# Turning the first MLP block's rows by crossbar DMA transposes instead of TensorE products and ScalarE copies

## The chip, the cores and the metric

The kernel runs on one core of a Trainium2 chip. The metric is the device time of one execution in microseconds (us). Engines are named as the profile names them: PE (TensorE products), PEld (its weight loads), DVE (VectorE), ACT (ScalarE), POOL (GpSimd) and SP (SyncE, which in this kernel only issues DMAs).

## The reference

Four residual layers run over 2048 tokens of width 576: attention, MLP, attention, MLP, with the same weights for both attention layers and for both MLP layers.

```python
def _A_ref(x, wqkv, wo):              # linear attention, 32 heads of 18
    q, k, v = split(x @ wqkv)
    phi = lambda t: jnp.where(t > 0, t + 1, jnp.exp(t)) + 1e-6
    kv = einsum("bhsd,bhse->bhde", phi(k), v);  z = phi(k).sum over s
    o = einsum(phi(q), kv) / (einsum(phi(q), z) + 1e-6)
    return o @ wo
def _B_ref(x, w1, b1, w2, b2):        # MLP, hidden width 4608
    y = _layernorm(x)
    return gelu(y @ w1 + b1) @ w2 + b2

x = A_x
x = x + _A_ref(_layernorm(x), A_wqkv, A_wo)
x = x + _B_ref(_layernorm(x), B_w1, B_b1, B_w2, B_b2)
x = x + _A_ref(_layernorm(x), A_wqkv, A_wo)
x = x + _B_ref(_layernorm(x), B_w1, B_b1, B_w2, B_b2)
```

Inputs, weights and output are bfloat16.

## The kernel before

**Layout.** Tokens lie in 16 row tiles of 128 (`t`), four of them make a block of 512 tokens (`c`). The layers are numbered from 1 here; the code's `li` counts from 0, so that layers 2 and 4 (the MLPs) are `li` 1 and 3, and the attention layers that feed them `li` 0 and 2. The products of each layer need the normalized rows with the width on the partitions: that is `yT`, five chunks of 128 by 2048 tokens. The fifth chunk has only 64 real values; for an MLP they are there twice, which is why GpSimd copies the last 64 columns of a normalized row once more behind them (L476).

**Row pipe.** `LNPipe` takes a residual row tile through stages, one stage a tick: statistics (stage 0, on DVE, or on ACT in two steps, L379 and L388), the reciprocal root (L433), a scale and shift (L436), the normalization into one of three row buffers `y_ring` (L466 where GpSimd does it), and then the turning of the row (stage 4). A tile can be made to `hold` for a number of ticks. There are two ways of turning. With `evac="act"` five TensorE transposes (L500) go to a PSUM bank `tp` and one ScalarE copy (L505) takes them to `yT`. With `evac="dma"` the rows are turned in 32x32 squares by VectorE into `turned`, stored to DRAM (L310), and fetched into place, a block of four tiles at a time.

**The handover from attention to MLP.** In the last stage of an attention layer `wo_stage(t)` makes the output product of row tile t in a pair of PSUM banks, `accA` for even t and `accB` for odd (L933), `residual` adds the old residual row `xo` on VectorE (L605), and the new row is stored to DRAM (L612). The old rows are loaded ahead by `prefetch_xo`, in layer 1 as pairs from the input (L575), in layer 3 one by one (L581), each into one of nine row buffers. Row tiles 0 to 3 go straight into the row pipe with `evac="act"`, normalized by GpSimd; their transposes come at an output row that is written out by hand (`tp_at`). One or two ticks follow each output row.

**The MLP.** For each block of 512 tokens, `m1_group` makes four hidden chunks at a time (L1045): two go to banks `h_ps` first, then two to a pair `hp_ps`, for which the banks `accA` and `accB` take turns, `accA` first. Each product takes all four row tiles of the block as its moving operand. Then the second product runs over all 36 hidden chunks for each row tile (L1104). Rows of blocks 1 to 3 are loaded again (L372) while the block before is computed, and are turned with `evac="dma"`.

**Order.** TensorE's order in the last attention stage and in the MLP is the program's, held by a chain of dependencies. On the other engines and on SP the tile framework's planner orders instructions by their dependencies and its own costs, within some orders set by hand. SP issues in that order and waits at each DMA for what it needs, so that a DMA that is not ready keeps those behind it back.

Of the kernel before, what the change touches and what calls it, by code (L numbers as in the profile page):

```python
# [15 lines left out]
P = 128  # L16
# [19 lines left out]
def build(tc, A_x, A_wqkv, A_wo, B_w1, B_b1, B_w2, B_b2, out, dbg=None, n_layers=4):  # L36
    nc = tc.nc
    dbg = dbg or {}
    with ExitStack() as ctx:
# [307 lines left out]
        class LNPipe:  # L347
# [11 lines left out]
            def tick(self, transposes=1):  # L359
                land()  # L360
                for it in list(self.items):
                    st = it["stage"]
                    if st == 4 and it["evac"] != "dma":
                        if transposes == 0 or state["wo"] < it["tp_at"]:
                            continue
                        transposes -= 1
# [57 lines left out]
                    elif st == 1:  # L424
                        rstd = work.tile([P, 1], F32, name="ln_rstd", bufs=6)
                        it["rstd"] = rstd
                        if "u" not in it:
                            named(f"ln{it['t']}", nc.scalar.activation(out=rstd[:], in_=it["mv"][:, 1:2], func=ACT.Ln,
                                                                       bias=eps_col[:, 0:1]))
                            named(f"re{it['t']}", nc.scalar.activation(out=rstd[:], in_=rstd[:], func=ACT.Exp, scale=-0.5))  # L430
                            it["stage"] = 2
                            continue
                        nc.gpsimd.tensor_tensor(out=rstd[:], in0=it["u"][:], in1=neg_half[:], op=ALU.pow)  # L433
                    elif st == 2 and it["norm"] != "dve":
                        nmr = work.tile([P, 1], F32, name="ln_nmr", bufs=4)
                        nc.gpsimd.tensor_scalar(out=nmr[:], in0=it["mv"][:, 0:1], scalar1=1.0 if it["stats"] == "act" else -1.0,  # L436
                                                scalar2=it["rstd"][:, 0:1], op0=ALU.mult, op1=ALU.mult)
                        it["nmr"] = nmr
                    elif st in (2, 3) and it["kind"] == "A" and it["evac"] == "act":
                        xt, t = it["xt"], it["t"]  # L440
                        tail = first_tail(t)[:, 0:64]
                        if it["norm"] == "pool":
                            for out, cols in ((xt[:, 0:4 * P], slice(0, 4 * P)), (tail, slice(4 * P, D))):
                                norm = nc.gpsimd.tensor_scalar(out=out, in0=xt[:, cols], scalar1=it["rstd"][:, 0:1],
                                                               scalar2=it["nmr"][:, 0:1], op0=ALU.mult, op1=ALU.add)
                            pool_last["norm"] = norm.ins.name
                        else:
                            for name, out, cols in ((f"n{t}", xt[:, 0:4 * P], slice(0, 4 * P)), (f"nt{t}", tail, slice(4 * P, D))):
                                norm = named(name, nc.vector.tensor_scalar(
                                    out=out, in0=xt[:, cols], scalar1=it["mv"][:, 0:1], scalar2=it["rstd"][:, 0:1],  # L450
                                    op0=ALU.subtract, op1=ALU.mult))
                            dve_last["norm"] = norm.ins.name
                        row_of[t] = xt
                        it["stage"] = 4
                        continue
                    elif st in (2, 3):
                        if sum(other["stage"] == 4 for other in self.items) == NY:
                            continue
                        y = y_ring[state["ycnt"] % NY]
                        state["ycnt"] += 1  # L460
                        xt = it["xt"]
                        if it["norm"] == "act":
                            nc.scalar.activation(out=y[:, 0:D], in_=xt[:, 0:D], func=ACT.Identity,
                                                 scale=it["rstd"][:, 0:1], bias=it["nmr"][:, 0:1])
                        elif it["norm"] == "pool":
                            norm = nc.gpsimd.tensor_scalar(out=y[:, 0:D], in0=xt[:, 0:D], scalar1=it["rstd"][:, 0:1],  # L466
                                                           scalar2=it["nmr"][:, 0:1], op0=ALU.mult, op1=ALU.add)
                            pool_last["norm"] = norm.ins.name
                        else:
                            norm = nc.vector.tensor_scalar(out=y[:, 0:D], in0=xt[:, 0:D], scalar1=it["mv"][:, 0:1],  # L470
                                                           scalar2=it["rstd"][:, 0:1], op0=ALU.subtract, op1=ALU.mult)
                            if it["after"] == "phi":
                                tc.add_manual_dep(norm.ins, dve_last["phi"], NOSYNC, reason="keys go on first")
                            dve_last["norm"] = norm.ins.name
                        if it["kind"] == "B" and it["evac"] != "dma":
                            nc.gpsimd.tensor_copy(out=y[:, D:DPAD], in_=y[:, 4 * P:D])  # L476
                        if it["kind"] == "A" and it["evac"] == "dma":
                            c, j = divmod(it["t"], TPC)
                            nc.sync.dma_start(out=yrow_d[c, :, j], in_=y[:, 0:D])
                        it["y"] = y  # L480
                        it["stage"] = 4
                        continue
                    elif st == 4:
                        t = it["t"]
                        first_layer = it["kind"] == "A" and it["evac"] == "act"
                        y = it["xt"] if first_layer else it["y"]
                        if it["evac"] == "dma":
                            turn_rows(y, t, it["kind"])
                            self.items.remove(it)
                            continue  # L490
                        tp = ps_h.tile([P, 512], F32, name="tp", tag="h")
                        tp = tp[:, 0:DPAD // 2].bitcast(BF16).rearrange("p (k n) -> p k n", k=KD)
                        first = first_layer and t < 2
                        tp2 = tp
                        if first:
                            tp2 = ps_h.tile([P, 512], F32, name="tp2", tag="h")
                            tp2 = tp2[:, 0:DPAD // 2].bitcast(BF16).rearrange("p (k n) -> p k n", k=KD)
                        for k in range(KD):
                            block = first_tail(t, P) if first_layer and k == 4 else y[:, k * P:(k + 1) * P]
                            pe(nc.tensor.transpose(out=(tp if k < 3 else tp2)[:, k, :], in_=block, identity=ident[:]))  # L500
                        if first:
                            named(f"ca{t}", nc.scalar.copy(out=yT[:, 0:3, t * P:(t + 1) * P], in_=tp[:, 0:3, :]))  # L502
                            named(f"cd{t}", nc.vector.tensor_copy(out=yT[:, 3:KD, t * P:(t + 1) * P], in_=tp2[:, 3:KD, :]))
                        elif it["evac"] == "act":
                            turned_tile = nc.scalar.copy(out=yT[:, :, t * P:(t + 1) * P], in_=tp)  # L505
                            act_last["turned"] = turned_tile.ins.name
                            if first_layer and t < 5:
                                named(f"ca{t}", turned_tile)
                            elif act_last["exp"] is not None:
                                tc.add_manual_dep(turned_tile.ins, act_last["exp"], NOSYNC, reason="keys go on first")  # L510
                        else:
                            nc.vector.tensor_copy(out=yT[:, :, t * P:(t + 1) * P], in_=tp)
                        self.items.remove(it)
                        continue
# [6 lines left out]
        lnp = LNPipe()  # L521
# [93 lines left out]
        def layer_A(li, next_kind, pre_a1=None):  # L615
# [321 lines left out]
            def wo_stage(t):  # L937
# [1 line left out]
                wp = wo_open[t][1]  # L939
                xn = residual(li, t, wp[:, :, 0:HALF])  # L940
                if xn is not None and next_kind == "B" and t < TPC:
                    lnp.feed(xn, t, "B", "pool", "act", hold=(2, 5, 6, 8)[t] if li > 0 else (2, 8, 8, 10)[t], tp_at=6 + 2 * t if li > 0 else (6, 10, 11, 14)[t],
                             **(dict(after="sum") if t in (0, 3 if li > 0 else 2) else dict(stats="act", after="rden")))

            for t in range(AHEAD if li == 0 else AHEAD + 2):
# [267 lines left out]
```

## Time and profile before

| | |
|---|---|
| device time, median of 3 runs | 760.16 us (760.14 to 760.37) |
| span of the profiled execution | 758.4 us |
| busy: PE, PEld | 753.2 us, 487.4 us |
| busy: ACT, DVE, POOL | 328.7 us, 272.0 us, 116.6 us |
| transposes of layer 2's and 4's first block (L500) | 40, median 218 ns |
| all copies from `tp` to `yT` by ACT (L505) | 22, median 687 ns (8 of them for these rows) |
| DMA | 73.90 MB, mean 97 GB/s |

The profile is of one execution, with times in us from the start of its span; the page gives no other time of its own for it, and the span is 1.8 us under the median. Busy times of engines overlap. A PE instruction's duration contains its way through the array, so the room that one takes in a row of products is the distance of two starts. In a timeline a row gives the start, the length, the engine, the line, the operation with its output and inputs, the count of merged instructions, and in brackets the idle time before it and what ended it.

### The profile page before, as it was taken

Reading aid. Unit: us, or ns where it says so; the run is one execution under the profiler, and the core shown is the slowest. Engines: PE = TensorE matmul, PEld = TensorE weight load, DVE = VectorE, ACT = ScalarE, POOL = GpSimd, SP = SyncE. Lnnn points to the kernel's source line nnn. Section 1 sums busy time; section 2 is a strip of 40 time slices with the busy share of each in tenths; the row PEclk is TensorE's granted clock in tenths of the full one; section 3 lists DMA queues with packets and bytes.
Section 4 is the critical chain, followed back from the end, with each engine's and each line's share of the span. In section 5 each row is a group of like instructions: output and inputs, shape, how many; then the busy total and the mean of one; then the engine's idle time right before and its main releaser. Section 6 shows DMA issues by size and latency. Waiting matters only on the chain.

```text
span 758.4 us, 15817 instructions
## 1 busy us (share of the span) xinstructions
PE 753.2 (99%) x6595; PEld 487.4 (64%) x6595; DVE 272.0 (36%) x685; ACT 328.7 (43%) x733; POOL 116.6 (15%) x196
## 2 busy tenths in 40 slices
PE   9999999999999999999999999999999999999998
PEld 5776754774477457646777777457646754774476
DVE  8876862136033503401367577600230131000000
ACT  6887656205600650263057666660174036205600
POOL 4840231002000301200100005300020020001000
PEclk9999999999999999999999999999999999999999
DMA  8994573026312711320404047530240033011000
GB/s 236 267 313 74 178 262 82 17 64 189 83 39 83 181 51 48 109 69 17 131 24 116 24 136 255 185 82 16 88 115 7 16 127 82 9 33 55 1 9 24
DMA packets 80977, 73.90 MB, mean 97 GB/s; under 512 B 36874, under 2 KB 65546, under 8 KB 80906
## 3 DMA queue, kind: packets, MB, share of 16 engines
q1 hardware_dynamic: 80906, 72.90, 33.0%
q8 instruction: 51, 0.84, 0.5%
q14 instruction: 20, 0.16, 0.1%
HBM read 48.10 MB, written 24.77 MB: 96 GB/s over the span
## 4 chain that ended last, share of the span: by engine, by line
PE 97%; DVE 1%; ACT 0%; issue 0%; DVEq 0%
PE m_ps L1104 36%; PE h_ps L1045 21%; PE hp_ps L1045 16%; PE q_ps L621 6%; PE k_ps L653 5%; PE wo_ps L933 5%; PE k_ps L678 4%; PE m_half L1104 1%; PE tp L500 1%; PE warm_ps L217 1%; PE k_tail L678 1%; PE kv_ps L719 0%; PE den_ps L769 0%; PE rden_ps L810 0%; PE kvwo_half L737 0%
## 5 line engine op out<-in xcount | busy, mean ns | idle before, releaser
L1104 PE MATMUL m_ps<-w_sb,hT 128*128 128x288 bf16 x2232 | 274.8, 286 | 0.0
L1104 PEld LDWEIGHTS <-hT 128*128 128x128 bf16 x2304 | 224.3, 98 | 60.4 <-issue 3.4
L1045 PEld LDWEIGHTS <-w_sb 64*128 64x128 bf16 x2304 | 124.5, 94 | 136.4 <-issue 1.9
L1045 PE MATMUL hp_ps<-yT,w_sb 64*128 64x512 bf16 x1152 | 178.0, 376 | 0.0
L1045 PE MATMUL h_ps<-yT,w_sb 64*128 64x512 bf16 x1152 | 148.0, 376 | 0.0
L1050 ACT COPY relay_sb<-relay_sb 128x1 f32<-128x1 f32 x144 | 28.5, 198 | 260.4 <-PE h_ps L1045 217.6
L1041 ACT ACTIVATE hT<-h_ps,b1T 128x512 bf16<-128x512 f32 x144 | 91.0, 683 | 44.1 <-PE h_ps L1045 44.1
L433 POOL TENSOR_TENSOR ln_rstd<-ln_u,neg_half 128x1 f32<-128x1 f32 x61 | 35.2, 577 | 439.9 <-DVE ln_u L415 218.0
L1041 ACT ACTIVATE hT<-hp_ps,b1T 128x512 bf16<-128x512 f32 x144 | 91.1, 692 | 0.0
L605 DVE TENSOR_TENSOR xbf<-m_ps,xo 128x576 bf16<-128x576 f32 x15 | 11.4, 757 | 213.5 <-PE m_ps L1104 213.5
L605 DVE TENSOR_TENSOR xo<-m_ps,xo 128x576 f32<-128x576 f32 x16 | 12.1, 757 | 172.6 <-PE m_ps L1104 172.6
L588 POOL TENSOR_TENSOR xo<-xo,b_bc 128x576 f32<-128x576 f32 x32 | 40.9, 1283 | 97.3 <-DMA xo<-x_d 58.4
L1045 PE MATMUL h_ps<-yT,w_tail 64*128 64x512 bf16 x144 | 54.1, 376 | 0.0
L1045 PE MATMUL hp_ps<-yT,w_tail 64*128 64x512 bf16 x144 | 54.1, 376 | 0.0
L621 PE MATMUL q_ps<-yT,wqkv_sb 128*126 128x512 bf16 (+1 forms) x200 | 49.3, 379 | 0.1
L653 PE MATMUL k_ps<-wqkv_sb,yT 128*128 128x288 bf16 x320 | 44.6, 286 | 0.2
L933 PE MATMUL wo_ps<-kvwo,pq 126*128 126x288 bf16 (+1 forms) x320 | 43.4, 286 | 0.3
L1045 PEld LDWEIGHTS <-w_tail 64*128 64x128 bf16 x288 | 27.1, 94 | 17.1
L653 PEld LDWEIGHTS <-yT 128*128 128x128 bf16 x320 | 31.0, 98 | 8.9 <-ACT yT L502 0.6
L933 PEld LDWEIGHTS <-pq 126*128 126x128 bf16 (+1 forms) x320 | 30.3, 97 | 9.1 <-issue 0.8
L621 PEld LDWEIGHTS <-wqkv_sb 128*126 128x126 bf16 (+1 forms) x200 | 25.7, 131 | 11.7 <-issue 0.5
L554 ACT ACTIVATE phi_e<-q_ps 126x512 bf16<-126x512 f32 (+1 forms) x40 | 23.9, 597 | 18.4 <-PE q_ps L621 16.8
(138 smaller groups left out, 591.6 us busy)
## 6 DMA issues: line engine op xcount, KB each, us to landing
xo<-x_d SPq DMA_DIRECT2D x48, 288.0 KB, 3.5
x_d<-xo SPq DMA_DIRECT2D x32, 288.0 KB, 2.6
xl<-x_d SPq DMA_DIRECT2D x24, 288.0 KB, 4.2
y_d<-turned SPq DMA_DIRECT2D x40, 144.0 KB, 3.1
w_sb<-in_B_w_dram SPq DMA_DIRECT2D x6, 864.0 KB, 10.4
yT<-y_d SPq DMA_DIRECT2D x10, 512.0 KB, 4.2
w_sb<-in_B_w_dram SPq DMA_DIRECT2D x9, 512.0 KB, 5.9
x_d<-xn SPq DMA_DIRECT2D x16, 288.0 KB, 3.3
```

The source lines that it names most:

```text
L433: nc.gpsimd.tensor_tensor(out=rstd[:], in0=it["u"][:], in1=neg_half[:], op=ALU.pow)
L554: exp = nc.scalar.activation(out=e_out, in_=ps_ap, func=ACT.Exp)
L588: nc.gpsimd.tensor_tensor(out=xo[:], in0=xo[:], in1=b2_bc[:], op=ALU.add)
L605: total = nc.vector.tensor_tensor(out=xn[:, cols].rearrange("p (h n) -> p h n", h=2), in0=halves, in1=xo[:, cols].rearrange("p (h n) -> p ...
L621: pe(nc.tensor.matmul(qp[0:GR[g], :], lhsT=wqkv_sb[:, k, GO[g]:GO[g] + GR[g]], rhs=yT[:, k, c * CA:(c + 1) * CA], start=(k == 0), stop=(k ...
L653: pe(nc.tensor.matmul(kp[:, 0:HALF], lhsT=yT[:, k, t * P:(t + 1) * P], rhs=wqkv_sb[:, k, D + half * HALF: D + (half + 1) * HALF], start=(k ...
L678: pe(nc.tensor.matmul(dst, lhsT=lhsT, rhs=pk, start=(t == 0), stop=(t == NT - 1)))
L933: pe(nc.tensor.matmul(wp[:, half, 0:HALF], lhsT=pq[(g, c)][0:GR[g], j * P:(j + 1) * P], rhs=kvwo[g][0:GR[g], half * HALF:(half + 1) * HALF ...
L1041: act_last["gelu"] = nc.scalar.activation(out=to, in_=ps, func=ACT.Gelu_apprx_tanh, bias=b1T[:, f:f + 1], scale=1.0).ins.name
L1045: mm = pe(nc.tensor.matmul(dst[n], lhsT=wt, rhs=mv, start=(seen[n] == 0), stop=(seen[n] == 8)))
L1050: relay = nc.scalar.copy(out=relay_sb[:, 1:2], in_=relay_sb[:, 0:1])
L1104: pe(nc.tensor.matmul(acc[half][:, 0:cols.stop - cols.start], lhsT=hT[f][:, j * P:(j + 1) * P], rhs=w2_sb[:, f, cols], start=(f == 0), sto ...
```

## The change

Row tiles 0 to 3 of layers 2 and 4 are handed to the row pipe with a new way of turning, `"xbar"`: one DMA transpose per row tile, issued on SP's queue from the row buffer (128 rows by 640 values) straight into the tile's 128 columns of the five chunks of `yT`. The gate that spaces the TensorE transposes (`tp_at`, and at most one per tick) does not apply to it. The TensorE transposes, the PSUM bank and the ScalarE copy of these rows fall away. For row tile 3 of layer 2 the hold is 9 ticks and not 10.

```diff
@@ LNPipe.tick
                     st = it["stage"]
-                    if st == 4 and it["evac"] != "dma":
+                    if st == 4 and it["evac"] not in ("dma", "xbar"):
                         if transposes == 0 or state["wo"] < it["tp_at"]:
                             continue
                         transposes -= 1
@@ LNPipe.tick, stage 4
                             turn_rows(y, t, it["kind"])
                             self.items.remove(it)
                             continue
+                        if it["evac"] == "xbar":
+                            nc.sync.dma_start_transpose(out=yT[:, :, t * P:(t + 1) * P], in_=y[:])
+                            self.items.remove(it)
+                            continue
                         tp = ps_h.tile([P, 512], F32, name="tp", tag="h")
@@ wo_stage
-                    lnp.feed(xn, t, "B", "pool", "act", hold=(2, 5, 6, 8)[t] if li > 0 else (2, 8, 8, 10)[t], tp_at=6 + 2 * t if li > 0 else (6, 10, 11, 14)[t],
+                    lnp.feed(xn, t, "B", "pool", "xbar", hold=(2, 5, 6, 8)[t] if li > 0 else (2, 8, 8, 9)[t], tp_at=6 + 2 * t if li > 0 else (6, 10, 11, 14)[t],
                              **(dict(after="sum") if t in (0, 3 if li > 0 else 2) else dict(stats="act", after="rden")))
```

More of the change, by code (lines that the diff above doesn't have):

```diff
@@ L941, in wo_stage @@
                 if xn is not None and next_kind == "B" and t < TPC:
-                    lnp.feed(xn, t, "B", "pool", "act", hold=(2, 5, 6, 8)[t] if li > 0 else (2, 8, 8, 10)[t], tp_at=6 + 2 * t if li > 0 else (6, 10, 11, 14)[t],
+                    lnp.feed(xn, t, "B", "pool", "xbar", hold=(2, 5, 6, 8)[t] if li > 0 else (2, 8, 8, 9)[t],
                              **(dict(after="sum") if t in (0, 3 if li > 0 else 2) else dict(stats="act", after="rden")))
```

## The prediction

> **What bounds the kernel now.** I read the shares and the chain on the page first, then the tile view of the transposes' PSUM tile `tp`, then the timelines of PE, POOL, SP and DVE around the two places where an attention layer hands over to an MLP layer (about 76 to 108 us and 447 to 480 us), and last DMA issues and stretches there.
>
> ```profile
> PE 753.2 (99%) x6595; PEld 487.4 (64%) x6595; DVE 272.0 (36%) x685; ACT 328.7 (43%) x733; POOL 116.6 (15%) x196
> PE 97%; DVE 1%; ACT 0%; issue 0%; DVEq 0%
> ```
> The chain is TensorE's, and TensorE is busy all through. So an instruction taken off PE can shorten the run, but only by the room it takes in PE's order, not by its own duration. The products that go, in the view of `tp` (minimum/median/maximum in ns; x40 is just those the change removes):
>
> ```profile
> L500 PE MATMUL tp<-ident,y_ring x40: 216/218/220, 88.7 to 469.7; 128*128 128x128 bf16 x40
> ```
> Their room is seen in PE's timeline (start, length, line, count), here layer 2's last output rows and the first group of the MLP:
>
> ```profile
> 100.14 0.44 PE L500 MATMUL tp<-ident,y_ring 128*128 128x128 bf16 x5
> 100.42 1.40 PE L933 MATMUL wo_ps<-kvwo,pq 126*128 126x288 bf16 x10
> 101.74 1.04 PE L1045 MATMUL h_ps<-yT,w_sb 64*128 64x512 bf16 x8
> ...
> 102.62 1.24 PE L1045 MATMUL hp_ps<-yT,w_sb 64*128 64x512 bf16 x8
> ```
> Five transposes start at 100.14 and the next product at 100.42: 0.28 us for the five. The MLP starts at 101.74 with `h_ps`; the pair bank `hp_ps` follows at 102.62. In layer 4 these two times are 473.56 and 474.44.
>
> **What is removed.** Start-to-start, the four groups of five take 0.27, 0.28, 0.27, 0.28 = 1.10 us of PE in layer 2, and 0.28, 0.27, 0.52, 0.28 = 1.35 us in layer 4 (the 0.52 holds a wait that is not the transposes' own: the next output product at 466.92 waits for VectorE's scaling of its queries). I take 1.10 us for each layer, 2.20 us in all, as the most that PE itself gives; with the waits near the transposes in layer 4 it could be 2.5. The skill has another price: the Trainium skill ("VectorE: DVE Perf Modes", The three transpose paths) gives 390 ns for one TensorE transpose of 128x128, by which forty would give back 15.6 us; the trace disagrees with 0.27 to 0.28 us for five in a row.
>
> ScalarE loses eight copies of 0.69 us. ACT is no link of the chain, but one copy stands ahead of a statistic that POOL waits for. In layer 2 the copy at 89.20 holds the second statistic of row tile 1 until 89.79; POOL then runs tiles 1 to 3 nearly back to back from 90.75. So all of it may come 0.59 us sooner. In layer 4 the same POOL work starts at 460.10, before that layer's first copy (460.38): nothing moves.
>
> **What is added.** Eight DMAs on SP's queue, each 128x640 bf16 = 160 KB, each waiting for POOL to finish its row (normalization, then the copy of the last 64 columns). The last one of each layer counts, for the MLP's first product reads columns of all four row tiles. POOL's last pieces:
>
> ```profile
> 98.53 0.24 POOL L476 COPY y_ring<-y_ring 128x64 bf16<-128x64 bf16 x1
> 468.65 0.24 POOL L476 COPY y_ring<-y_ring 128x64 bf16<-128x64 bf16 x1
> ```
> Row tile 3 is thus ready at 98.77 in layer 2 (98.18 with the 0.59) and at 468.89 in layer 4. Before, 3.0 and 4.7 us were left to the MLP's start, and transpose plus copy took one of them. Now a DMA must land in it. The shortened hold of tile 3 in layer 2 (10 to 9 ticks) puts its first statistic one tick earlier; POOL has tile 2 until 96.20 and starts tile 3 at 96.36, so it gives at most 0.16 us, taken as nothing. If POOL were free there it would be a full tick, about 0.7 us. The wider condition at the transposes' gate only lets the new kind through at once. The freed `tp` banks help nobody in view: no wait in the two windows is on them.
>
> No crossbar transpose is in this trace, so its time from issue to landing is bounded by other DMAs (count, KB, median us to landing; the fourth row is from layer 4's window, the others from the whole run):
>
> ```profile
> out_dram<-xbf SPq DMA_DIRECT2D x15, 144.0 KB, 1.8
> y_d<-turned SPq DMA_DIRECT2D x40, 144.0 KB, 3.1
> yT<-y_d SPq DMA_DIRECT2D x16, 64.0 KB, 5.4
> xo<-x_d SPq DMA_DIRECT2D x10, 288.0 KB, 5.5
> ```
> I take 3.1 us in layer 2: nearest size, and also a shuffle in small pieces. The DMA share there is still moderate, but in layer 4 the engines are full (last columns: clock, DMA share, GB/s):
>
> ```profile
> 96.00:100.00 4.00, 4.00 (x37) 3.20 (x36) 2.30 (x4) 1.44 (x4) 2.25 (x6) 1.00 0.54 165
> 468.00:472.00 4.00, 4.00 (x37) 3.10 (x36) 2.46 (x4) 0.69 (x1) 0.82 (x2) 1.00 0.95 308
> ```
> *Layer 2.* Ready 98.18, issued about 98.5 (SP is sending stores then), landed 98.5 + 3.1 = 101.6. PE would be there at 101.74 - 1.10 = 100.64. So the MLP starts at 101.6: -0.1 us. With 1.8 us it lands at 100.3 and all 1.10 is kept; with 5.4 it lands at 103.9, +2.2.
>
> *Layer 4.* Here a second wait lies just behind PE:
>
> ```profile
> 468.62 0.32 SPq L581 DMA_DIRECT2D xo<-x_d  x1
> 469.05 0.37 SPq L612 DMA_DIRECT2D x_d<-xo  x1
> 469.52 0.37 SPq L581 DMA_DIRECT2D xo<-x_d  x1
> 470.24 4.27 SPq L612 DMA_DIRECT2D x_d<-xo  x5
> 473.40 0.76 DVE L605 TENSOR_TENSOR xo<-wo_ps,xo 128x576 f32<-128x576 f32 x1 [1.39 <-DMA xo<-x_d]
> ```
> The residual row of tile 14 is loaded at 468.62 (its buffer comes free with POOL's normalization of tile 3, ended 468.59) and lands at 473.40, 4.8 us later. Its sum ends at 474.16 and frees the bank `accA`, which `hp_ps` takes at 474.44. If PE comes 1.10 us sooner, `hp_ps` still waits for this sum: a gain of at most 0.2 us is left, not 1.10. The transpose of tile 3 is issued behind that load at about 469.1, and with the same 4.8 us lands at 473.9, +0.3. The transpose of tile 2 (row ready 466.30) goes ahead of the load: its 160 KB at 308 GB/s are 0.5 us, which make load, sum and `hp_ps` 0.5 later. Both agree on about +0.5. Bounds: -0.2 with 1.8 us and no crowding; with 5.5 us, tile 3 lands at 474.6, +1.0.
>
> Queued behind a waiting transpose on SP are the stores of later rows (L612), residual loads (L575, L581) and the MLP's first row loads (L372). Tiles 0 and 1 wait for rows that are ready 10 us and more ahead of the MLP in layer 4 (456.93, 463.24), 8 us in layer 2; they cost nothing unless they hold SP. The row loads serve the MLP's second block, 70 us later, and are covered. The three-deep ring of normalized rows is no wait: tile 3 takes tile 0's place at 97, tile 0 having been issued by 87.
>
> **Sum.** Layer 2 -0.1, layer 4 +0.5: +0.4 us. The profiled span is 758.4; the runs' median of 760.16 is 1.8 above, which I take as unchanged: 758.8 + 1.8 = 760.6. By the bounds alone: -1.1 - 0.2 = -1.3 to +2.2 + 1.0 = +3.2.
>
> **Rivals.** *Both layers keep PE's gain.* Layer 2 gives 1.10 and layer 4 its 1.10 too: 758.0. With the waits around, 757.7. For it: PE has no other gap in layer 2. Against it: in layer 4 tile 14's load must come 0.9 us sooner, and POOL, which releases it, is not relieved there. The planner may give that load another buffer, since rows 5 and 6 were stored long before. Chance 0.15.
>
> *A transpose holds SP.* If SP can't go on to its next DMA until the crossbar has taken the transpose, tile 2's keeps the load of tile 14 back. SP has room: the store at 466.33 is done at 467.48 and the load goes at 468.62, 1.1 us. From a hold over 1.1 us on, all excess goes to that load, its sum and `hp_ps`. With a hold as long as that stretch's landing, 4.8 us from 466.4, the load goes at 471.2, +2.6: 762.8 with layer 2 unchanged. For it: stores issued in a row already follow each other by 0.85 us (5 in 4.27) against 0.37 alone. Against it: no issue alone is long here. Chance 0.27, at 761.7 to 764.
>
> *The crossbar goes block by block.* If the five 128x128 blocks of a row follow one another, each at the pace of a whole small DMA at its fastest (1.8 us), a row takes 9 us: layer 2 lands at 107.5, +5.8, layer 4 at 478.1, +4.5, 770.5; if blocks overlap by half, about 765.3. Against it: 40 stores of `turned` with smaller pieces take 3.1. The Trainium skill, in the same section, gives 1309 ns for one 128x128 on the crossbar and its rules for kernel authors prefer TensorE where PSUM will do; an estimate from it, five in a row, is 6.5 us, or 765.5 by the same working. No row here shows either. Chance 0.13.
>
> *It isn't a crossbar transpose*, but a copy in 2-byte pieces: 81,920 pieces a row, far beyond any range. Chance 0.02.
>
> **The numbers.** The forecast's case keeps 0.43, from 758.7 to 761.7. A measurement can tell about 0.2%, 1.5 us, from no change, so that case is the "same": 0.43. Faster is only the first rival, 0.15; slower the other three, 0.42. The range runs from 758.0 to 764.0: it leaves out some 0.05 of the first rival and the 0.15 of the last two.
>
> **What would show it.** PE's row for `tp` falls by 40 and ACT's copies to `yT` by 8. The MLP of layer 2 starts at about 101.6, after a DMA; layer 4's start to `hp_ps` is 0.5 late behind tile 14's sum. A landing under 2 us in both, or a sum of tile 14 before 473, makes me wrong on the fast side; SP idle behind a transpose for over 1.1 us, or a landing over 6 us, on the slow side.

## The result, and the profile after

The changed kernel takes 768.33 us (median of 4 runs, 766.83 to 769.93) against 760.26 us: slower by 1.05%, ratio 1.0105 with a 95% interval of 1.0088 to 1.0122. The forecast was 760.6 us in a range of 758.0 to 764.0. It was wrong: the time lies above the range. In the runs of 766.83 and 767.25 us the mean granted clock of PE is 1.0, in the other two it is 0.998.

One line of the diff above is misquoted. In the changed kernel the call of `feed` no longer passes `tp_at`. For `"xbar"` nothing reads it, so the change itself is as described; but where an experiment turns one layer back to TensorE, `tp_at` has to come back with it (see the fourth run).

The profiled execution of after is the run of 766.83 us, with a span of 765.1 us, 6.7 above before's. Engines and chain on its page:

```profile
PE 751.8 (98%) x6555; PEld 487.4 (64%) x6555; DVE 269.2 (35%) x685; ACT 323.9 (42%) x725; POOL 117.0 (15%) x196
PE 94%; DMA 2%; DVE 1%; ACT 1%; issue 1%; POOL 0%; SPq 0%; DVEq 0%; POOLq 0%
```

PE has lost its 40 transposes and ACT its 8 copies, as the prediction said. But the chain, which was PE to 97%, now holds DMAs. PE's timeline shows where it stands idle (last bracket: idle time and what ended it), first in layer 2, then in layer 4. Line numbers after the change are 4 higher.

```profile
93.54 3.86 PE L937 MATMUL wo_ps<-kvwo,pq 126*128 126x288 bf16 x30 [1.42 <-DVE xn L609]
97.90 1.39 PE L937 MATMUL wo_ps<-kvwo,pq 126*128 126x288 bf16 x10 [0.50 <-DVE xn L609]
99.63 3.86 PE L937 MATMUL wo_ps<-kvwo,pq 126*128 126x288 bf16 x30 [0.34 <-DVE xn L609]
105.87 1.04 PE L1049 MATMUL h_ps<-yT,w_sb 64*128 64x512 bf16 x8 [2.39 <-issue]
...
475.64 1.39 PE L937 MATMUL wo_ps<-kvwo,pq 126*128 126x288 bf16 x10 [1.33 <-DVE xo L609]
478.17 1.39 PE L937 MATMUL wo_ps<-kvwo,pq 126*128 126x288 bf16 x10 [1.14 <-DVE xo L609]
480.26 1.04 PE L1049 MATMUL h_ps<-yT,w_sb 64*128 64x512 bf16 x8 [0.70 <-DMA yT<-y_ring]
```

The MLP of layer 2 starts at 105.87 and not at 101.74 (+4.13); layer 4's at 480.26 and not at 473.56 (+6.70, so +2.57 of its own). Two kinds of idle time make this up: waits inside the output stage, for sums (2.26 us in layer 2, 2.47 in layer 4), and the wait ahead of the MLP (2.39 and 0.70). Each wait also costs the overlap of the products on its two sides, about 0.15 us: ten products alone take 1.39 us, thirty in a row 3.86. In layer 2 four waits thus come to 4.65 + 0.6 us; less the 1.10 us of the transposes that are gone, this is about the 4.13. In layer 4, with 1.35 us gone, the same sum gives 2.3 of the 2.57 us. SP's timeline in layer 2 shows the first kind at its root, first before the change, then after it:

```profile
83.88 0.38 SPq L575 DMA_DIRECT2D xo_pair<-in_A_x_dram  x1
85.38 1.97 SPq L612 DMA_DIRECT2D x_d<-xn  x2
...
95.92 0.38 SPq L575 DMA_DIRECT2D xo_pair<-in_A_x_dram  x1
```

```profile
82.06 1.72 SPq L616 DMA_DIRECT2D x_d<-xn  x2
86.11 1.34 SPq L492 DMA_TRANSPOSE yT<-y_ring  x1
88.00 0.40 SPq L579 DMA_DIRECT2D xo_pair<-in_A_x_dram  x1
88.51 0.96 SPq L616 DMA_DIRECT2D x_d<-xn  x2
...
99.70 0.43 SPq L579 DMA_DIRECT2D xo_pair<-in_A_x_dram  x1
100.23 0.46 SPq L616 DMA_DIRECT2D x_d<-xn  x1
100.78 2.35 SPq L492 DMA_TRANSPOSE yT<-y_ring  x1
```

The planner put row tile 0's transpose ahead of a load and two stores. It waits for POOL until 86.08 and then holds SP for 1.34 us; the pair of stores that began at 85.38 before now begins at 88.51, the load of 83.88 goes at 88.00, and the load of 95.92, now behind two more transposes, at 99.70. Row buffers come free late, and DVE's sums wait for DMAs:

```profile
92.73 0.76 DVE L609 TENSOR_TENSOR xn<-wo_ps,xo_pair 128x576 f32<-128x576 f32 x1 [1.58 <-DMA x_d<-xn]
104.38 1.42 DVE L609 TENSOR_TENSOR xn<-wo_ps,xo_pair 128x576 f32<-128x576 f32 x2 [2.40 <-DMA xo_pair<-in_A_x_dram]
```

The second kind is the landing. In layer 4 the chain names it:

```profile
475.91 4.30 DMA yT<-y_ring
480.21 0.05 issue
480.26 1.25 PE h_ps L1049 x9
```

In layer 2 the chain says only "issue"; the first product started 5.09 us after the transpose's issue at 100.78. The trace also keeps the events of the semaphores that DMAs count up when they land. By these the transpose landed at 105.67, 4.89 us after its issue and 0.20 us ahead of the product. The last sum on VectorE ended at 105.80, nearer still, but it is not what PE waits for: in run 1 below, the sums were done at 104.9, the last transpose landed at 107.54, and PE started at 107.63.

### The profile page after: what moved, and what is told of

It is laid out like the page before. It is cut to its first block, busy times and chain, and to the rows that moved or that the text cites. A ratio compares the mean times of both kernels' runs of the same rounds, so it can differ in the third digit from the quotient of the medians.

```text
span 765.1 us, 15754 instructions
## 1 busy us (share of the span) xinstructions
PE 751.8 (98%) x6555; PEld 487.4 (64%) x6555; DVE 269.2 (35%) x685; ACT 323.9 (42%) x725; POOL 117.0 (15%) x196
## 4 chain that ended last, share of the span: by engine, by line
PE 94%; DMA 2%; DVE 1%; ACT 1%; issue 1%; POOL 0%; SPq 0%; DVEq 0%; POOLq 0%
PE m_ps L1108 36%; PE h_ps L1049 20%; PE hp_ps L1049 16%; PE q_ps L625 6%; PE k_ps L657 5%; PE k_ps L682 4%; PE wo_ps L937 3%; PE m_half L1108 1%; ACT turned L818 1%; DMA yT<-y_ring 1%; PE k_tail L682 1%; PE tp L504 0%; DMA x_d<-xn 0%; DMA xo<-x_d 0%; PE rden_ps L814 0%
## 5 line engine op out<-in xcount | busy, mean ns | idle before, releaser
L1049 PEld LDWEIGHTS <-w_sb 64*128 64x128 bf16 x2304 | 126.5, 94 | 137.5 <-issue 4.1
```

The source lines that it names most:

```text
L1049: mm = pe(nc.tensor.matmul(dst[n], lhsT=wt, rhs=mv, start=(seen[n] == 0), stop=(seen[n] == 8)))
```

## The experiments

Theory 1: SP's single queue. A transpose waits there for POOL and then holds the queue, so that stores and loads behind it come late. Theory 2: the landing of the last transpose ahead of the MLP. Theory 3: the crossbar's traffic slows all DMAs. All times are medians, with the ratio to the kernel before (760.1 to 760.4 in the same sessions).

**1. The transposes on ScalarE's DMA queue.**

```diff
-    nc.sync.dma_start_transpose(out=yT[:, :, t * P:(t + 1) * P], in_=y[:])
+    nc.scalar.dma_start_transpose(out=yT[:, :, t * P:(t + 1) * P], in_=y[:])
```

> The eight transposes are issued on ScalarE's DMA queue and not on SP's; SP's order of DMAs is then that of the kernel before. Theory 1 (SP's queue: a transpose waits there for POOL and then holds the queue about 1.3 us, so stores, residual loads and the sums behind them come late): the waits inside the output stage (about 2.4 us of PE idle in layer 2, 2.5 in layer 4) go, what is left is the wait for the last landing; 761 to 764 us. Theory 2 (the loss is the last transpose's landing ahead of the MLP, 2.4 us idle in layer 2 and 0.7 in layer 4, whichever queue): the wait ahead of each MLP stays as it is, and the time falls by what the stage's idle was, only if that idle was SP's doing; with landing alone 766 to 768. Theory 3 (the crossbar's traffic slows the other DMAs): as the change, 767 to 769.

773.61 us, ratio 1.0179 (1.0151 to 1.0207): worse than the change, and no theory gave it. SP was free, but the same wait and hold now stood in ScalarE's own order. Its timeline, and PE's beside it:

```profile
86.05 1.31 ACTq L492 DMA_TRANSPOSE yT<-y_ring  x1
87.40 2.05 ACT L818 CAST turned<-rden_ps 126x512 bf16<-126x512 f32 x4 [3.43 <-issue]
```

```profile
88.03 0.38 PE L798 MATMUL rden_ps<-quad_rden,head_bc 128*128 128x512 bf16 x1 [1.90 <-ACT turned L818]
```

PE waits 6.6 us in all for ScalarE's copies of the denominators, and 3.51 us for the landing in layer 2. So a transpose that waits and holds was costly on this queue too; as ScalarE's own delays moved the whole stage, this run does not part the theories.

**2 and 3. Eight DMAs added to the kernel before, which nobody waits for**: as transposes, then as plain copies.

```diff
+    if st == 4 and it["kind"] == "B" and it["evac"] == "act" and not it.get("sent"):
+        it["sent"] = True
+        nc.sync.dma_start_transpose(out=yT[:, :, (it["t"] + TPC) * P:(it["t"] + TPC + 1) * P], in_=it["y"][:])
         # third run instead: nc.sync.dma_start(out=dead_d[layer, it["t"]], in_=it["y"][:])
```

> The kernel before, with its TensorE transposes and copies kept, and the same eight DMA transposes added on SP's queue, into columns of yT that nothing reads before they are written again: nobody waits for their landing. Theory 1: the loss inside the output stages comes back without any landing to wait for, +3 to +6 us, 763 to 766. Theory 2: within 0.5 us of the kernel before, 760 to 761. Theory 3: 763 to 766 as theory 1, told apart by dead_copy.

> As dead_xbar, but the eight added DMAs are plain copies of the same 160 KB rows to a DRAM buffer that nothing reads. If it is the wait for POOL at the head of SP's queue that costs, they cost as much as the dead transposes (763 to 766). If it is the transposes' hold on the queue (1.24 to 2.35 us each, plain DMAs 0.35 to 0.5), they cost less than half of it (760.5 to 762.5). If it is bytes on the DMA engines, as much as the transposes.

Transposes: 765.11 us, ratio 1.0071 (1.0055 to 1.0087), +4.95 us. Plain copies: 762.32 us, ratio 1.0027 (1.0018 to 1.0037), +2.2 us. With nobody waiting for a landing, the stalls of the output stage are there again, in layer 2 and in layer 4:

```profile
93.60 2.62 PE L936 MATMUL wo_ps<-kvwo,pq 126*128 126x288 bf16 x20 [1.28 <-DVE xn L608]
...
476.76 1.39 PE L936 MATMUL wo_ps<-kvwo,pq 126*128 126x288 bf16 x10 [1.14 <-DVE xo L608]
```

So theory 1 carries 5 of the 8 us, and theory 2 alone falls. The plain copies pay 44% of it. They have the same bytes and wait for POOL at similar places, but hold SP for much less. The two rows are from the line views of the dead copies and of the changed kernel (ns, minimum/median/maximum):

```profile
L366 SPq DMA_DIRECT2D dead_d<-y_ring x8: 319/344/416, 86.4 to 471.4; - x8
...
L492 SPq DMA_TRANSPOSE yT<-y_ring x8: 1238/1319/2355, 86.1 to 475.9; - x8
```

The larger part is thus the transpose's own, its hold on SP or its way over the DMA engines; the smaller is a DMA of that size waiting at the head of the queue.

The semaphore events of the kept traces part the two. If the crossbar's traffic slowed the DMAs around it, they would land later after their issue. In layer 2's output stage (81 to 103 us) a store of a row takes 3.57 us from issue to landing on the mean in the kernel before, 3.64 with the dead transposes, 3.60 with the dead copies and 3.74 in the change; a load of old rows takes 3.90, 3.66, 3.68 and 3.74. In layer 4's (454 to 482 us) no mean is over 0.2 us above that of before. What differs is when they are issued: the store that the first late sum waits for goes at 88.97 with the dead transpose ahead of it and at 88.18 with the dead copy, in a run whose stage began 0.28 us later. With that taken off, it goes 1.07 us later, about the difference of the two holds (1.34 and 0.32). So theory 3 does not hold for these DMAs, and the transpose's own part points to its hold on SP.

**4. Layer 2 alone, first form.** Only the argument was changed, so layer 4's TensorE transposes had lost `tp_at`.

```diff
-    lnp.feed(xn, t, "B", "pool", "xbar", ...
+    lnp.feed(xn, t, "B", "pool", "xbar" if li == 0 else "act", ...
```

> Crossbar transposes in layer 2 alone, layer 4 as in the kernel before. The profiles of before and after put the MLP's start of layer 2 at 101.74 and 105.87, that of layer 4 6.70 later: if the two layers add, this one costs 4.1 us (764.3) and layer 4's would cost 2.6. If layer 4's loss is a consequence of layer 2's (another order of buffers), this costs all 6.7 (767).

770.12 us, ratio 1.0126 (1.0109 to 1.0142). It says nothing on layer 4's crossbar transposes: without `tp_at` PE waited 4.5 us for POOL at the four groups of TensorE transposes there. It showed something else in layer 2. The MLP began after 3.16 us of idle, and the clock granted to PE then fell (stretches; the third number from the right is the clock):

```profile
106.00:112.00 6.00, 5.63 (x38) 2.67 (x40) 1.77 (x6) 1.24 (x4) 0.86 (x2) 0.72 1.03 391
112.00:118.00 6.00, 6.00 (x59) 3.11 (x57) 5.63 (x11) 4.33 (x10) 2.73 (x3) 1.00 0.43 165
```

**5 and 6. One layer each**, with `tp_at` and the old holds for the other.

```diff
-    lnp.feed(xn, t, "B", "pool", "xbar", ...
+    lnp.feed(xn, t, "B", "pool", "xbar" if li == 0 else "act", ..., tp_at=...   # sixth run: li > 0
```

> Crossbar transposes in layer 2 alone; layer 4 has its TensorE transposes at the output rows of before (the run only_l2 had lost that spacing, so this one takes its place). If the two layers add, 764.3 us, by the MLP's start of 101.74 before and 105.87 after; if PE's clock falls after the wait for the last landing, as in the profile of only_l2 (0.72 between 106 and 112 us after 3.16 us of idle), 1.5 to 2 us more, 766.

> Crossbar transposes in layer 4 alone. l2_alone cost 5.4 us of the change's 8.1: if the layers add, this costs 2.6 us by the profiles (6.70 less 4.13) to 2.8: 762.7 to 763.2. More than 764 would mean that the layers do not add.

Layer 2: 765.55 us, ratio 1.0067 (1.0052 to 1.0082), +5.4. Layer 4: 763.44 us, ratio 1.0042 (1.0029 to 1.0056), +3.1. Together 8.5 against 8.1 for both: the layers add, and each has its own loss. Layer 4's run holds a fall of the clock too: in its profile (764.68 us) the MLP begins at 0.61 of the clock for 4.4 us, behind waits of 1.13, 1.35 and 0.85 us.

**7. Each transpose behind a later store.**

```diff
+    if st == 4 and it["evac"] == "xbar" and state["wo"] < it["xb_at"]:
+        continue
...
-    nc.sync.dma_start_transpose(...)
+    turn = nc.sync.dma_start_transpose(...)
+    tc.add_manual_dep(turn.ins, sp_last["store"], NOSYNC, reason="rows behind stores")
...
+    xb_at=(5, 8, 11, 12)[t] if li > 0 else (6, 9, 11, 12)[t]
```

> All eight transposes stay on SP, but each is placed behind a later store (of row tile 6, 9, 11, 12 in layer 2, of 5, 8, 11, 12 in layer 4), so that no store or load waits behind a transpose that is itself waiting for POOL, and the loads for the last rows go first. Theory 1 (queue order): the idle inside the output stages goes, some 2 us a layer; what stays is the wait for the last landing, 3 to 4 us ahead of layer 2's MLP and about 1 in layer 4, with the clock's fall where the idle passes 3 us: 762 to 766. If the transposes cost by their hold and their traffic wherever they stand in the queue: 767 to 770.

773.91 us, ratio 1.0181 (1.0165 to 1.0196), far above both expectations. The place of the idle came out as theory 1 has it: inside both output stages PE waits 0.4 us in all. But all of it, and more, moved to the landing: 4.38 us ahead of layer 2's MLP and 6.09 us ahead of layer 4's, and behind each wait the clock is halved. The row gives 1.89 us for products that took 1.04 before:

```profile
105.66 1.89 PE L1052 MATMUL h_ps<-yT,w_sb 64*128 64x512 bf16 x8 [4.38 <-DMA yT<-y_ring]
...
105.60:110.00 4.40, 4.34 (x22) 1.88 (x24) 1.69 (x5) 0.38 (x2) 1.09 (x2) 0.50 1.06 409
110.00:114.00 4.00, 4.00 (x36) 1.86 (x32) 3.64 (x9) 2.50 (x5) 1.47 (x3) 0.85 0.60 214
```

So neither of the two orders tried is good for four transposes a layer: early, they keep back the loads; late, they keep back the MLP. That no order between them is good is not shown.

**8. The same, with idle products in the waits**: 18 in layer 2, 26 in layer 4, on TensorE ahead of each MLP.

```diff
+    warm_pe_again(18 if li == 0 else 26)   # matmuls of w2_sb by w2_sb into a spare bank
```

> As ordered4, with idle products put on TensorE ahead of each MLP (18 in layer 2, 26 in layer 4, 0.22 us each, fewer than the waits of 4.4 and 6.1 us hold): their results are not used. If the fall of PE's clock to 0.50 for 4.4 us behind each wait is a matter of the idle time, the clock stays at 1.0, each MLP's first groups take 1.9 us less, and the time falls from 773.9 to 769.5 to 771. If the landing of the transposes had come later for a reason that slows TensorE too, it stays at 773 to 775.

768.87 us, ratio 1.0111 (1.0095 to 1.0126): 5.0 us less by adding work. The clock stays up:

```profile
105.85 1.04 PE L1058 MATMUL h_ps<-yT,w_sb 64*128 64x512 bf16 x8 [0.39 <-DMA yT<-y_ring]
...
105.00:109.40 4.40, 4.01 (x37) 1.93 (x36) 1.18 (x4) 0.85 (x3) 0.28 (x1) 1.00 1.06 407
```

In run 7 the clock was 0.50 from 105.66 to 111.2 us in layer 2 and from 485.85 to 490.1 in layer 4. Half of these 5.5 and 4.25 us is lost, 4.9 together, which is the 5.0 within the spread of the runs.

**9. Idle products in the change itself**, ten of them, ahead of layer 2's MLP only.

```diff
+    if li == 0:
+        warm_pe_again(10)
```

> The change with ten idle products (2.2 us, unused results) put on TensorE ahead of layer 2's MLP, inside the wait for the last landing (2.39 us in its profile). The change's four runs were 766.8, 767.3 with a mean granted clock of 1.0 and 769.4, 769.9 with 0.998. If the upper two are runs in which this wait passed 3 us and the clock fell, all runs are now 766.5 to 767.5. If the fall happens in layer 4 (waits of 1.33, 1.14 and 0.70 us between single rows of products), the two groups of times stay.

767.95 us, ratio 1.0096 (1.0079 to 1.0113); two runs at 767.1 and 767.5 with clock 1.0, two at 768.4 and 768.6 with 0.997 and 0.998. The two groups stay, so in this kernel the fall is not layer 2's alone. Its profile has it in layer 4 (0.80 between 476 and 481 us), after waits of 1.58 and 0.90 us with one row of products between them.

**10. Tile 3 by TensorE, tiles 0 to 2 by the crossbar.**

```diff
-    lnp.feed(xn, t, "B", "pool", "xbar", ...
+    lnp.feed(xn, t, "B", "pool", "xbar" if t < 3 else "act", ..., tp_at=...
```

> Row tiles 0 to 2 by the crossbar as in the change, tile 3 of each layer by TensorE and ScalarE as before. No MLP waits for a late landing. Theory 1: the stalls of the output stage stay as in dead_xbar (765.1) less three tiles' PE time in each layer (1.65 us), 763 to 764.5. Theory 2 (the landing is the loss): 758.5 to 760.

764.67 us, ratio 1.0069 (1.0046 to 1.0092), five runs from 763.2 to 768.7. No MLP waits for a transpose to land, and 4.5 us of loss remain: theory 1's number, 0.2 us above its upper end (one run of the five, the profiled one, holds a fall of the clock). Layer 2's MLP starts at 103.72, but its second pair of banks then waits for the sum of row tile 14:

```profile
103.72 1.04 PE L1049 MATMUL h_ps<-yT,w_sb 64*128 64x512 bf16 x8
...
105.91 1.04 PE L1049 MATMUL hp_ps<-yT,w_sb 64*128 64x512 bf16 x8 [0.95 <-DVE xn L609]
```

That sum's load went at 99.25, behind the transposes, and took 5.73 us. In the change the same load goes at 99.70 and the sum ends at 105.14. A transpose landing at once would thus have won some 1.5 us of layer 2's 2.39 (`hp_ps` at about 105.2 and not 106.75, an estimate from these rows), not all of them.

**11 and 12. Only transposes that fit where SP stood idle before.** With the code of run 7, tile 0 of each layer; then tile 1 of layer 2 as well.

```diff
-    lnp.feed(xn, t, "B", "pool", "xbar", ...
+    lnp.feed(xn, t, "B", "pool", "xbar" if t == 0 else "act", ..., xb_at=6 if li == 0 else 5,
     # twelfth run: t == 0 or (t == 1 and li == 0), xb_at=(6, 8)[t] in layer 2
```

> Only row tile 0 of each layer by the crossbar, placed behind the store of row tile 6 (layer 2) and 5 (layer 4), where SP stood idle before; the other three by TensorE. If the cost is queue order and late landing, none is left and PE gains 0.55 us: 759.4 to 760.0. If a transpose costs by its mere hold and traffic, 0.5 us or more each: 760.5 to 762.

> Row tile 0 of both layers and tile 1 of layer 2 by the crossbar, each placed where SP stood idle in the profile of before (behind the stores of row tiles 6 and 8 in layer 2, of 5 in layer 4), the others by TensorE. Three groups of five products go, 0.27 us each, and a wait of some 0.2 us ahead of one in layer 4: 759.1 to 759.6 us if a well-placed transpose is free; first_late (two of them) had 759.43. Over 760.1 if tile 1's transpose delays the load for tiles 14 and 15 behind it.

Two transposes: 759.43 us, ratio 0.9992 (0.9983 to 1.0002), not told from no change. Three: 759.24 us against 760.37, ratio 0.9986 (0.9977 to 0.9995): the one version that beats both kernels, by 1.1 us with the interval clear of 1. In its SP timeline layer 2's transposes stand in what was idle time, and the load behind the second one goes at 95.67, no later than before (95.92, when POOL had done with its row buffer):

```profile
91.16 1.38 SPq L494 DMA_TRANSPOSE yT<-y_ring  x1
...
94.27 1.31 SPq L494 DMA_TRANSPOSE yT<-y_ring  x1
95.67 0.53 SPq L582 DMA_DIRECT2D xo_pair<-in_A_x_dram  x1
```

## Why the prediction was wrong, point by point

- **PE's share of the removal: right.** 0.27 us for five transposes: the three groups of the twelfth run, 0.8 us by that price, came back as 1.1 us, with an interval of 0.4 to 1.7. ACT's relief moved nothing that lasts: row tile 1 was ready sooner (92.03 and not 93.75), but POOL's rows of tiles 2 and 3 became later.
- **"They cost nothing unless they hold SP" (tiles 0 and 1): the step that failed.** It looked at when their rows are needed, not at what stands behind them in SP's order. The transposes were put ahead of stores and loads, where they waited for POOL and then held SP. The condition behind "unless" was the case. The dead transposes price it at 4.95 us, where the sum had 0.5 us, for tile 2 in layer 4 alone. (Tile 0's row in layer 4 was ready at 457.23; the 456.93 of the text is where its last copy starts. Nothing hangs on it.)
- **The rival "a transpose holds SP" had the mechanism and the threshold, but too small a price and chance.** The holds are 1.24 to 2.36 us, just over its 1.1. It followed only tile 14's load in layer 4 (762.8). In fact layer 2, given as unchanged, lost more (5.4 us alone), for the stores there free the buffers of the next sums. "No issue alone is long here" was read from plain DMAs of layer 4; in layer 2 of the same trace a plain store had held SP for 2.53 us, at 96.91, inside a merged row.
- **Ready and issue of the last row in layer 2.** The text had the row ready at 98.18 and issued at 98.5. It was ready at 99.78, because tile 2's statistic came at 93.64 and not 91.94, behind the late sum, and it was issued at 100.78. These are consequences of the step above. Issued at 98.5, as the text had it, a landing of 4.89 us would have put the MLP at 103.4, 1.7 us late and inside the bounds.
- **The landing.** 3.1 us were taken in layer 2 and 4.89 measured; in run 7 the chain has 4.16 us for the same transpose. In layer 4 4.8 were taken and 4.30 measured. All are inside the bounds of 1.8 to 5.5. The Trainium skill ("Advanced Engine Details and Errata", X-Bar Transpose (TRN2)) calls these transposes as fast as regular DMAs: in landing the trace roughly agrees (4.30 us; the load at 471.52 took 3.23 us, the one at 468.62 before 4.8, each with 288 KB and not 160); in the issuer's time it does not, 1319 against 344 ns.
- **The crossbar block by block: not borne out.** By the semaphore events the eight landings of the change took 2.67 to 4.89 us. Over all runs they go from 2.63 to 6.24 us on SP's queue and to 7.10 on ScalarE's (run 1), so no fixed 9 or 6.5 us a row shows.
- **PE's clock: in no rival.** Half the runs of the change have a mean clock of 0.998 and are 2.6 us above the others on the mean (769.7 against 767.0). The profiled one is not among them, so for the change itself the link is by these means only; runs 4, 7 and 8 show the fall.

What stays open: why the last transpose of layer 2 held SP for 2.35 us and the others for 1.24 to 1.36, and what filled the 0.20 us between its landing and the first product. That the hold and not the traffic makes the 2.8 us between dead transposes and dead copies rests on the times of issue and landing, not on a run that changes the one without the other.

## What to carry to other kernels

A DMA that waits for an engine is an instruction in its issuer's order, so list what stands behind it before asking when its own data is needed; here that list cost 5 us where the data itself had 8 us to spare. Moving work from a busy engine to "free" DMAs paid here only in the issuer's own gaps: three transposes in such gaps won 1.1 us, eight in the planner's order lost 8. And price an idle PE at more than its length when it passes 3 us, or when shorter waits follow each other closely.

## What the runs showed of the hardware that was not expected

- A crossbar transpose of 160 KB holds its issuing queue for 1.24 to 2.36 us in the change, on SP and on ScalarE's queue (1.22 to 1.90, run 1) alike; a plain copy of the same row holds it for 0.32 to 0.42 us (run 3). The DMAs around the transposes land no later for them: stores 3.57 us after issue before, 3.64 with dead transposes.
- PE's granted clock was 0.50 for the first 5.5 and 4.25 us of the MLPs behind waits of 4.38 and 6.09 us (run 7), and it fell behind 3.16 (run 4) and 3.51 us (run 1); behind 2.31 (run 5), 2.39 (the change) and 2.86 us (run 1, layer 4) it did not. Products whose results are dropped kept it up. The Trainium skill ("TensorE: Matmul & The Clock Gate", Why this matters for your kernels) warns of PE gaps over about 3 us, with half the clock behind them: for a single gap the runs agree. They add that shorter waits close together can do it too (1.58 and 0.90 us in run 9, 1.19 and 1.45 us in run 10), but need not (1.33, 1.14 and 0.70 us in the profile of the change).
